# Scores of the first two pairs of heads as float32 in 64-row tiles, and small steps moved between engines

## The chip, the cores and the metric

The kernel runs on one core of a Trainium2 chip. The metric is the device time of one execution in microseconds (us). The program is written with an explicit order of instructions for each engine: TensorE (PE, with its weight loads PEld), VectorE (DVE), ScalarE (ACT), GpSimd (POOL) and SyncE (SP), which issues the DMAs.

## The reference, cut to what matters

```python
def _attn_ref(q, k, v, tau):                      # 8 batches, 8 heads, 576 rows, 64 wide
    scores = (1.0 / np.sqrt(64)) * np.matmul(q, k.transpose(0, 1, 3, 2))
    thresh = np.max(scores, axis=-1, keepdims=True) - tau
    scores = np.where(scores >= thresh, scores, -1e9)
    attn = np.exp(scores - np.max(scores, axis=-1, keepdims=True))
    attn = attn / (np.sum(attn, axis=-1, keepdims=True) + 1e-9)
    return np.matmul(attn, v)
def _moe_ref(x, mu_k, mu_r, w_k, w_v, w_r):       # x is 8 x 576 x 512, d_ff 1024
    xk = mu_k * x + (1 - mu_k) * x_prev           # x_prev: one row earlier
    xr = mu_r * x + (1 - mu_r) * x_prev
    k = np.maximum(xk @ w_k, 0.0)
    return 1 / (1 + np.exp(-(xr @ w_r))) * (k * k @ w_v)
def _moe2_ref(x, w_val, conv_w, w_out):           # causal convolution over 5 rows
    gate = 1 / (1 + np.exp(-conv(x, conv_w)))
    return gate * (x @ w_val) @ w_out
```

The five weight matrices and conv_w arrive as float64 and are converted on the chip.

## The kernel before, in words

**Attention.** The 64 heads are taken as 32 pairs; a pair has nine chunks of 128 query rows: eight of one head each (`c` from 0 to 7, the head alternating) and a ninth, `both`, that holds the last 64 rows of both heads. `prep` (from L392) loads q and k of a head with the 64 dimensions standing twice, on partitions 0 to 63 and 64 to 127. ScalarE rounds q (L409) and k (L405) to float32r, GpSimd subtracts in one half of the rows so that this half holds q's remainder (L419), and VectorE makes k's remainder `kl` (L413). The score of a chunk is then, for each half of the 576 keys (288), the sum of two float32r matmuls over all 128 rows, with k and with `kl` (`qk`, L462), into two PSUM banks. k carries the factor -1/8, so the scores are negated.

VectorE takes the minimum of the 576 scores of each row (L472), GpSimd adds tau to it (the threshold, L475), ScalarE exponentiates (L485), VectorE masks by the threshold and sums the row (L494). In the first six pairs (`LATE_PAIRS`) the sums of a half pair are collected in a tile `ss`; `guard_all` (L623, VectorE) adds 1e-9, `recip_all` (L628) inverts, GpSimd widens (L633), TensorE turns the result (L642) and the output is scaled (L647, L649). In the later pairs each chunk has its own guard (L499), reciprocal (L504) and a normalisation of P on GpSimd (L507).

P is transposed by TensorE. In pairs 0 to 3 (`COPY_FROM = 4`) directly, as float32 (L533); from pair 4 on a DMA first copies the P tile of two chunks into a tile `pr` (`move`, L561; two such tiles, `PRS`) and the transposes read that as float32r (L531). ScalarE brings the turned P back to SBUF (L544, L547, L552). TensorE multiplies it with V in float32: the two heads of a pair as two 64-column halves of the array (L597), the last keys of both in one piece (L600).

**Feed-forward.** `moe1` works on ten blocks of 464 rows: `mix_k` makes xk as a float32r value and a remainder, and the products with w_k and w_v are sums of three float32r matmuls (all at L674, in `mm3`). The first block needs the attention output of all four pairs of the first batch. `block2` does the same for w_r, w_val and w_out, with the convolution (L979), when the attention is over.

**Weights.** `split_weight` loads a 128 x 512 block of float64 as two 32-bit halves. `to_f32` (from L304) then makes a float32 of it in five steps: ScalarE scales the upper half read as float32 (L313), VectorE shifts it left by 3 (L316), VectorE puts the sign bit in (`sign`, L319), ScalarE scales the lower half (L323), GpSimd adds the two as integers (L326). ScalarE rounds the result to float32r (L353), and GpSimd or VectorE makes the remainder (L356). There are 28 such blocks: 8 of w_k and 8 of w_v early, 12 of the other three during the attention, and once a small one for conv_w.

**Order.** Nothing is scheduled by hand: every step is given to `Plan.op` with an engine, a guessed duration, its dependences and a priority, and `Plan.order` simulates the engines and buffers (tokens) and fixes the order in which each engine's instructions stand. All constants from L186 on are parameters of that plan: priorities and guessed durations. SyncE's one queue issues all loads, stores and copies in that order, and an issue that waits for its data holds back those behind it. The lines from L237 to L258 come ahead of the plan: the loads of `par` (identity, mixing factors, tau) and of `conv_w`, and a few small operations.

```python
    def op(self, eng, dur, fn, deps=(), prio=0.0, acq=(), rel=(), lat=0.0, port=False):
    ...
        deps = [last.get("qk")] + [o for hd in ((0, 1) if both else (head,)) for o in qk_done[pi, hd]]
    ...
        mx = op("dve", 670, least, (o,), e, acq=("sm",))
        th = op("pool", 260, thr, (mx,), at - THR_EARLY)
        e1 = chain("exp", op("act", 625, ex, (mx, last.get("exp")), e, acq=("p",) if head == 0 else ()))
        mk = op("dve", 821, mask, (e1, th), e, acq=("ss",) if late and c in (0, 4) else (),
```

## Time and profile before

| | |
|---|---|
| Time, median of 3 runs | 1241.86 us (1238.85 to 1243.0) |
| The profiled execution | 1238.36 us, span of its instructions 1236.5 us |
| Mean granted TensorE clock | 0.996 |
| Busy: PE, PEld | 1195.4 us (97%), 1015.8 us (82%) |
| Busy: DVE, ACT, POOL | 923.8 us (75%), 838.9 us (68%), 681.8 us (55%) |
| Chain that ended last | PE 77%, DVE 7%, DMA 6%, ACT 4%, POOL 3%, issue 3% |

The shares of the span are averages over stages that differ: attention of the first batch alone, attention beside the first feed-forward, and the second feed-forward alone. The matmul records are pipelined: a record lasts longer than the distance to the next one, so the pace is read from the starts. A line of the form "x16" in the timeline merges 16 instructions.

### The profile page before, as it was taken

How to read it: one execution, taken by the hardware profiler on the slowest of the kernel's cores; microseconds unless marked ns; L12 is line 12 of the kernel's file. 1: busy time of each engine (PE TensorE's matmuls, PEld its weight loads, DVE VectorE, ACT ScalarE, POOL GpSimd, SP SyncE). 2: the span in 40 equal slices, each digit the busy share in tenths (PEclk: the TensorE clock that was granted, in tenths of full speed). 3: DMA queues.
4: the chain of work that ended last, by engine and by line, in shares of the span. 5: the costliest groups of instructions: out<-in, count | busy, mean ns of one | idle time of the engine just before them, and what ended most of it. 6: DMA issues, size and time to landing. Idle time of an engine off the chain costs nothing.

```text
span 1236.5 us, 21250 instructions
## 1 busy us (share of the span) xinstructions
PE 1195.4 (97%) x7134; PEld 1015.8 (82%) x7134; DVE 923.8 (75%) x2029; ACT 838.9 (68%) x1609; POOL 681.8 (55%) x914
## 2 busy tenths in 40 slices
PE   5889999999999999999999999999999999999998
PEld 4667778887878788888887888888888888888887
DVE  7999988998888898798897876862425985555450
ACT  7899867887777776786876676753535775555442
POOL 5676766676566667566666474540306764444331
PEclk9989999999999999999999999999999999999999
DMA  7346545566646556555556455325106332221111
GB/s 251 119 145 229 205 175 214 206 234 234 230 168 227 214 204 227 195 185 206 210 203 237 158 180 179 151 114 202 63 16 238 109 123 93 93 93 64 38 38 62
DMA packets 71501, 201.91 MB, mean 163 GB/s; under 512 B 10848, under 2 KB 28384, under 8 KB 70624
## 3 DMA queue, kind: packets, MB, share of 16 engines
q1 hardware_dynamic: 71392, 200.55, 45.7%
q8 instruction: 57, 0.93, 0.3%
q14 instruction: 52, 0.43, 0.1%
HBM read 91.48 MB, written 34.73 MB: 102 GB/s over the span
## 4 chain that ended last, share of the span: by engine, by line
PE 77%; DVE 7%; DMA 6%; ACT 4%; POOL 3%; issue 3%; SPq 0%; DVEq 0%; POOLq 0%; ACTq 0%
PE g L674 51%; PE s L462 10%; PE g L597 8%; PE g L531 6%; DMA pr<-p 4%; PE g L600 3%; DVE p L494 2%; DVE sm L472 2%; ACT p L485 1%; DVE kl L413 1%; POOL sm L475 1%; POOL p L507 1%; ACT pt L544 1%; DMA raw<-in_qkb 0%; DMA stage<-in_w_r 0%
## 5 line engine op out<-in xcount | busy, mean ns | idle before, releaser
L507 POOL TENSOR_SCALAR p<-p,sm 128x576 f32<-128x576 f32 x234 | 192.3, 827 | 129.6 <-DVE sm L504 92.6
L472 DVE TENSOR_REDUCE sm<-s 128x1 f32<-128x576 f32 x288 | 212.2, 749 | 56.1 <-PE s L462 54.5
L485 ACT ACTIVATE p<-s,sm 128x576 f32<-128x576 f32 x288 | 211.5, 750 | 62.2 <-DVE sm L472 41.7
L494 DVE SCALAR_TENSOR_TENSOR p<-s,sm,p 128x576 f32<-128x576 f32 x288 | 229.1, 811 | 28.3 <-ACT p L485 18.6
L462 PE MATMUL s<-qkh 128*128 128x288 f32 x640 | 206.2, 337 | 14.5 <-ACT qkh L409 8.7
L462 PE MATMUL s<-kl,qkh 128*128 128x288 f32 x640 | 181.7, 299 | 0.1
L475 POOL TENSOR_SCALAR sm<-sm,gs 128x1 f32<-128x1 f32 x288 | 110.7, 386 | 107.2 <-DVE sm L472 62.9
L544 ACT ACTIVATE pt<-g 128x512 f32<-128x512 f32 x256 | 140.9, 603 | 29.4 <-PE g L531 27.5
L462 PEld LDWEIGHTS s<-qkh 128*128 128x128 f32 x640 | 122.7, 192 | 23.6 <-POOL qkh L419 9.2
L597 PE MATMUL g<-pt,v 128*64 128x320 f32 (+1 forms) x1024 | 139.7, 414 | 0.0
L531 PEld LDWEIGHTS g<-ident_r,pr 128*128 128x128 f32 (+1 forms) x1148 | 112.6, 140 | 19.4 <-issue 3.5
L462 PEld LDWEIGHTS s<-kl,qkh 128*128 128x128 f32 x640 | 123.0, 192 | 5.5 <-DVE kl L413 0.7
L531 PE MATMUL g<-ident_r,pr 128*128 128x128 f32 (+1 forms) x1148 | 118.6, 243 | 8.0 <-DMA pr<-p 7.0
L674 PE MATMUL g<-kh,w_v_hi 128*128 128x464 f32 x320 | 121.8, 380 | 0.0
L674 PE MATMUL g<-xkh,w_k_hi 128*128 128x464 f32 x320 | 120.9, 378 | 0.1
L674 PE MATMUL g<-xkh,w_k_lo 128*128 128x464 f32 x320 | 119.6, 374 | 0.0
L674 PE MATMUL g<-kh,w_v_lo 128*128 128x464 f32 x320 | 119.2, 372 | 0.0
L597 PEld LDWEIGHTS g<-pt,v 128*64 128x64 f32 x1024 | 68.8, 137 | 53.3 <-issue 11.5
L419 POOL TENSOR_TENSOR qkh<-raw,qkh 64x576 fp32r<-64x576 f32 x64 | 95.1, 1486 | 20.3 <-ACT qkh L409 8.6
L979 DVE SCALAR_TENSOR_TENSOR g<-y,cw_t,g 128x464 f32<-128x464 f32 x160 | 104.0, 700 | 1.2 <-ACT g L976 0.5
L937 DVE TENSOR_TENSOR y<-gate,vt 128x464 f32<-128x464 f32 x40 | 31.8, 801 | 74.8 <-ACT gate L932 73.4
L1011 POOL TENSOR_TENSOR gvl<-gate,gvh 128x464 fp32r<-128x464 f32 x40 | 48.3, 1208 | 70.2 <-ACT gvh L1008 70.2
(108 smaller groups left out, 2669.4 us busy)
## 6 DMA issues: line engine op xcount, KB each, us to landing
pr<-p SPq DMA_DIRECT2D x112, 576.0 KB, 3.5
raw<-in_qkb SPq DMA_DIRECT2D x32, 640.0 KB, 4.7
raw<-in_qka SPq DMA_DIRECT2D x32, 608.0 KB, 4.3
v<-in_vp SPq DMA_DIRECT2D x32, 320.0 KB, 3.1
x_d<-x SPq DMA_DIRECT2D x32, 290.0 KB, 4.0
v_d<-vo SPq DMA_DIRECT2D x40, 232.0 KB, 2.5
vt<-v_d SPq DMA_DIRECT2D x10, 928.0 KB, 4.6
pr<-p SPq DMA_DIRECT2D x28, 288.0 KB, 3.5
```

Source lines behind the costliest of these rows:

```text
L419: nc.gpsimd.tensor_tensor(out=t["hi"][lo_rows, qs], in0=t["raw"][lo_rows, qs], in1=t["hi"][lo_rows, qs].bitcast(F32), op=ALU.subtract)
L462: nc.tensor.matmul(s_t[g][:, hh, 0:NT], lhsT=q, rhs=k, start=(i == 0), stop=(i == len(terms) - 1))
L472: nc.vector.tensor_reduce(out=sm[:, 0:1], in_=s_t[g][:, :, 0:NT], op=ALU.min, axis=AX.XY)
L475: nc.gpsimd.tensor_scalar(out=sm_t[g][:, 1:2], in0=sm_t[g][:, 0:1], scalar1=tau_t, scalar2=1.0, op0=ALU.add, op1=ALU.mult)
L485: nc.scalar.activation(out=view(), in_=s_t[g][:, :, 0:NT], func=AF.Exp, bias=sm_t[g][:, 0:1], scale=-1.0)
L494: nc.vector.scalar_tensor_tensor(out=view(), in0=s_t[g][:, :, 0:NT], scalar=sm[:, 1:2], in1=view(), op0=ALU.is_le, op1=ALU.mult, accum_out=to)
L507: nc.gpsimd.tensor_scalar(out=view(), in0=view(), scalar1=sm_t[g][:, 3:4], scalar2=1.0, op0=ALU.mult, op1=ALU.mult)
L531: nc.tensor.transpose(o_.bitcast(F32R), in_=i_.bitcast(F32R), identity=ident_r)
L544: nc.scalar.activation(out=pt[:, head, :, q0:q0 + 128], in_=ps.rearrange("p (k q) -> p k q", k=4), func=AF.Copy)
L597: nc.tensor.matmul(acc[h * 64:h * 64 + 64, 0:n], lhsT=v[:, kc * 128 + h * 64:kc * 128 + h * 64 + 64], rhs=pt[:, h, kc, 0:n], start=(kc == ...
L674: nc.tensor.matmul(ps()[:, 0:TW], lhsT=W[w][wt][:, kc, m * 128:(m + 1) * 128].bitcast(F32R), rhs=a(at, kc), start=(i == 0 and x == 0), sto ...
L979: nc.vector.scalar_tensor_tensor(out=f["ps"], in0=t["y"][:, c, k:k + TW], scalar=cw[:, c, k:k + 1], in1=f["ps"], op0=ALU.mult, op1=ALU.add)
```

## The change: what it does, and the diff

- **Float32 scores.** For the first two pairs (`RAW_TO = 2`), q and k are loaded straight into the tile that TensorE reads, without rounding: q stands on both halves of the partitions as before, but on partitions 0 to 63 lies the first half of the keys and on 64 to 127 the second (the host lays that out), so only 288 or 352 columns of k are loaded and scaled. A chunk's scores are two float32 matmuls, each over 64 rows of the array, one on the upper and one on the lower rows (`qk_f32`). The four steps L409, L405, L413 and L419 fall away in these pairs; one scaling of k is left.
- **Signs.** In `to_f32` the shift falls away as a step of its own. GpSimd multiplies the upper half, read as float32, by zero, which leaves a signed zero (`zero`), and VectorE shifts and ors in one operation (`join`). The zero doesn't wait for ScalarE's scaling.
- **Guards.** `guard_all` goes from VectorE to GpSimd.
- **Copies.** `COPY_FROM` goes from 4 to 1: P of pairs 1 to 3 is copied too, and turned as float32r.
- **Loads.** `par` and `conv_w` are loaded from ScalarE's queue.
- **Plan.** Instructions have a mode, a change of mode costs `SWITCH` in the simulation, and chunks of the new mode may be ganged; the simulated DMA queue starts earlier; many constants have new values.

```diff
-EARLY, QK_EARLY, T_LATE, EV_EARLY, AV_LATE = 3.8603, 0.3303, -0.4166, 23.5198, 0.3289
+EARLY, QK_EARLY, T_LATE, EV_EARLY, AV_LATE = 4.2537, 0.3178, -0.4775, 98.9593, 0.4182
-MOE_LAG = 0.4706
-MOE_STEP = 0.8177
+MOE_LAG = 0.5251
+MOE_STEP = 0.8168
-COPY_FROM = 4
+COPY_FROM = 1
-MIX_EARLY, SIDE_EARLY = 4.2746, 0.1496
-W_KEY, W_STEP = -1.8366, 23.7965
-V_KEY, V_STEP = 1.1975, -0.1648
+MIX_EARLY, SIDE_EARLY = 6.4759, 0.2235
+W_KEY, W_STEP = 0.6869, 171.2624
+V_KEY, V_STEP = 1.6325, -0.7381
-VAL_LAG, OUT_LAG = 1.5867, 2.6821
-LATE2, LOAD2, MIX2, CONV_LAG, THR_EARLY = -0.8579, -49.8364, 0.8009, 207.2935, 184.052
-MIX_AT = 72.9433
-OUT_FETCH = 182.6794
-PORT_TOL, PORT_SLACK = 623.2361, 1.4633
+VAL_LAG, OUT_LAG = 2.8855, 4.4173
+LATE2, LOAD2, MIX2, CONV_LAG, THR_EARLY = 14.1984, 54.2671, 6.5168, 421.219, 1653.4806
+MIX_AT = 24.4154
+OUT_FETCH = 341.8965
+PORT_TOL, PORT_SLACK = 494.0914, 1.91
+SWITCH = 200.0
+GANG = 2.4021
+RAW_TO = 2
+DMA_FROM = 500.0
...
-    nc.sync.dma_start(out=par_t, in_=par)
+    nc.scalar.dma_start(out=par_t, in_=par)
...
-    nc.sync.dma_start(out=cw_raw, in_=conv_w)
+    nc.scalar.dma_start(out=cw_raw, in_=conv_w)
...
-        def shift():
-            nc.vector.tensor_scalar(out=bits, in0=fi, scalar1=3, scalar2=None, op0=ALU.logical_shift_left)
-
-        def sign():
-            nc.vector.scalar_tensor_tensor(out=bits, in0=fi, scalar=-2147483648, in1=bits,
-                                           op0=ALU.bitwise_and, op1=ALU.bitwise_or)
+        def zero():
+            nc.gpsimd.tensor_scalar(out=bits.bitcast(F32), in0=halves[:, :, 1].bitcast(F32), scalar1=0.0, scalar2=1.0,
+                                    op0=ALU.mult, op1=ALU.mult)
+
+        def join():
+            nc.vector.scalar_tensor_tensor(out=bits, in0=fi, scalar=3, in1=bits,
+                                           op0=ALU.logical_shift_left, op1=ALU.bitwise_or)
...
+        if pi < RAW_TO:
+            end = 640 + RAW_KW[head]
+
+            def load_f32():
+                t["hi"] = qk_t[pi, head] = qk_p.tile([128, w], F32R, name="qkh", tag="qkh")
+                nc.sync.dma_start(out=t["hi"][:, 0:end].bitcast(F32), in_=src[b, p][:, 0:end])
+
+            def scale_k():
+                k = t["hi"][:, 640:end].bitcast(F32)
+                nc.scalar.activation(out=k, in_=k, func=AF.Copy, scale=g_s)
+            o = dma(512 * end, load_f32, (), prio, acq=("qk",), more=700)
+            qk_done[pi, head] = (chain("cast", op("act", 400 + 53 * head, scale_k, (o, last.get("cast")), prio)),)
+            return
...
+        def qk_f32():
+            s_t[g] = (pool["s3"] if s_tok == "s3" else s_p).tile([128, 2, 512], F32, name="s", tag="s")
+            heads = (0, 1) if both else (head,)
+            for hd in heads:
+                t = qk_t[pi, hd].bitcast(F32)
+                q = (512, 0)[hd] if both else QO[hd] + j * 128
+                k = 640 + (64 if both and hd else 0)
+                for x in (0, 1):
+                    r = slice(64 * x, 64 * x + 64)
+                    nc.tensor.matmul(s_t[g][:, x, 0:NT], lhsT=t[r, q:q + 128], rhs=t[r, k:k + NT],
+                                     start=(hd == heads[0]), stop=(hd == heads[-1]))
...
                 def guard_all():
                     ss = ss_t[pi, half]
-                    nc.vector.tensor_scalar(out=ss[:, 0:n_s], in0=ss[:, 0:n_s], scalar1=1e-9, scalar2=1.0,
+                    nc.gpsimd.tensor_scalar(out=ss[:, 0:n_s], in0=ss[:, 0:n_s], scalar1=1e-9, scalar2=1.0,
                                             op0=ALU.add, op1=ALU.mult)
...
-                o = op("dve", 90, guard_all, masks, e, port=True)
+                o = op("pool", 240, guard_all, masks, e)
```

## Rows read from the trace of the kernel before

**Rows 1.** Windows of the core: stretch, length, busy PE, PEld, DVE, ACT, POOL, clock, DMA, GB/s.

```profile
0.00:11.10 11.10, 2.24 (x5) 1.31 (x5) 3.93 (x8) 5.58 (x9) 3.59 (x7) 1.00 0.77 262
11.10:44.00 32.90, 25.12 (x161) 20.00 (x160) 32.62 (x64) 29.90 (x57) 21.94 (x31) 1.00 0.61 201
44.00:113.30 69.30, 59.75 (x412) 45.97 (x412) 68.77 (x140) 61.41 (x121) 47.16 (x69) 0.95 0.48 165
113.30:310.00 196.70, 192.78 (x1263) 159.60 (x1264) 175.62 (x426) 153.67 (x302) 135.72 (x193) 0.99 0.60 210
310.00:1236.50 926.50, 915.49 (x5298) 788.94 (x5296) 642.82 (x1395) 588.29 (x1123) 473.36 (x615) 1.00 0.42 151
```

**Rows 2.** Timeline of PE, 100 to 125 us: start, duration, instruction; the first at L674.

```profile
113.28 0.48 PE L674 MATMUL g<-xkh,w_k_hi 128*128 128x464 f32 x1
```

**Rows 3.** Timeline of all engines, 0 to 22 us: the opening.

```profile
0.74 0.40 SPq L237 DMA_DIRECT2D par_t<-in_par  x1
...
1.66 0.42 SPq L402 DMA_DIRECT2D raw<-in_qka  x1
...
6.34 0.74 ACT L409 ACTIVATE qkh<-raw 128x640 fp32r<-128x640 f32 x1 [2.28 <-DMA raw<-in_qka]
...
8.67 0.61 PE L462 MATMUL s<-qkh 128*128 128x288 f32 x1 [8.67 <-ACT qkh L409]
...
11.11 0.74 DVE L472 TENSOR_REDUCE sm<-s 128x1 f32<-128x576 f32 x1
```

**Rows 4.** Groups by line and shape, whole span: count, busy us, mean ns, idle before.

```profile
L507 POOL TENSOR_SCALAR p<-p,sm 128x576 f32<-128x576 f32 x234 | 192.3, 827 | 129.6 <-DVE sm L504 92.6 <-DVE sm L499 35.2
...
L475 POOL TENSOR_SCALAR sm<-sm,gs 128x1 f32<-128x1 f32 x288 | 110.7, 386 | 107.2 <-DVE sm L472 62.9 <-DVE sm L499 15.7 <-ACT p L485 9.5
...
L419 POOL TENSOR_TENSOR qkh<-raw,qkh 64x576 fp32r<-64x576 f32 x64 | 95.1, 1486 | 20.3 <-ACT qkh L409 8.6 <-issue 6.2 <-POOL sm L475 1.8
...
L597 PE MATMUL g<-pt,v 128*64 128x320 f32 x512 | 76.8, 443 | 0.0
...
L597 PE MATMUL g<-pt,v 128*64 128x256 f32 x512 | 62.9, 385 | 0.0
...
L409 ACT ACTIVATE qkh<-raw 128x640 fp32r<-128x640 f32 x64 | 48.1, 751 | 4.4 <-DMA raw<-in_qka 2.3 <-PE s L462 1.7 <-DMA raw<-in_qkb 0.4
...
L405 ACT ACTIVATE qkh<-raw,gs 128x576 fp32r<-128x576 f32 x32 | 25.2, 788 | 0.0
```

**Rows 5.** Windows of L316 alone (the shift): stretch, length, DVE busy, clock, DMA, GB/s.

```profile
11.10:113.30 102.20, 9.99 (x12) 0.97 0.52 176
```

**Rows 6.** Windows of L623 alone (the guard on VectorE), the same columns.

```profile
11.10:113.30 102.20, 5.24 (x9) 0.97 0.52 176
```

**Rows 7.** Windows of L413 alone (the remainder of k), the same columns.

```profile
11.10:113.30 102.20, 10.20 (x11) 0.97 0.52 176
```

**Rows 8.** The tile pr, 95 to 160 us: its copies by DMA, from issue to landing.

```profile
DMA to landing us min/median/max: 2.3/3.7/7.2
```

**Rows 9.** Timeline of PE, 20 to 100 us: scores, products with V, scores.

```profile
57.23 0.29 PE L462 MATMUL s<-qkh 128*128 128x288 f32 x1
57.37 0.29 PE L462 MATMUL s<-kl,qkh 128*128 128x288 f32 x1
57.59 2.38 PE L597 MATMUL g<-pt,v 128*64 128x320 f32 x16
59.89 0.81 PE L600 MATMUL g<-ptl,v 128*128 128x320 f32 x2
60.30 0.54 PE L462 MATMUL s<-qkh 128*128 128x288 f32 x1
60.67 0.30 PE L462 MATMUL s<-kl,qkh 128*128 128x288 f32 x1
```

**Rows 10.** Timeline of PE: eight transposes as float32 (L533) and as float32r (L531).

```profile
68.95 1.04 PE L533 MATMUL g<-par_t,p 128*128 128x128 f32 x8
...
117.37 0.84 PE L531 MATMUL g<-ident_r,pr 128*128 128x128 f32 x8
```

More of the change, by code (lines that the diff above doesn't have):

```diff
@@ L46 @@
 QKW = (KO[0] + KW[0], KO[1] + KW[1])
+RAW_KW = (288, 352)
 NCH = 9
@@ L88, in order @@
         n = 0
-        port = 0.0
+        port, mode = 0.0, 0
         cold, runs = True, []
-        busy["dma"] = 1400.0
-        heapq.heappush(events, (1400.0, -1, "idle", None))
+        busy["dma"] = DMA_FROM
+        heapq.heappush(events, (DMA_FROM, -1, "idle", None))
         def push(t, kind, o):
@@ L139, in order @@
                             skipped.append(held)
+                    if e == "pe" and mode == 1 and pick is not None and pick.mode != 1:
+                        late = pick.prio + GANG
+                        while ready[e]:
+                            x = heapq.heappop(ready[e])
+                            if x[2].mode == 1 and x[0] <= late and all(free[t] > 0 for t in x[2].acq):
+                                skipped.append((pick.prio, pick.idx, pick))
+                                pick = x[2]
+                                break
+                            skipped.append(x)
+                            if x[0] > late:
+                                break
                     for x in skipped:
@@ L157, in order @@
                     if e == "pe":
+                        if pick.mode != mode:
+                            pick.dur += SWITCH
+                        mode = pick.mode
                         while runs and runs[0][1] < now - WARM:
@@ L326, in add @@
             nc.gpsimd.tensor_tensor(out=bits, in0=bits, in1=fi, op=ALU.add)
-        return scale, shift, sign, low, add
+        return scale, zero, join, low, add
     for f in to_f32(cw_raw, cw_t[:, 0, :].bitcast(I32), cw_t[:, 1, :]):
@@ L1064 @@
     qkb = np.concatenate([bb, bb], 2)
+    kr = np.concatenate([kb[..., 512:], kb], -1)
+    for i in range(RAW_TO):
+        i = divmod(i, NP)
+        for x in (0, 1):
+            qka[i][64 * x:64 * x + 64, 640:640 + RAW_KW[0]] = ka[i][:, x * NT:x * NT + RAW_KW[0]]
+            qkb[i][64 * x:64 * x + 64, 640:640 + RAW_KW[1]] = kr[i][:, x * NT:x * NT + RAW_KW[1]]
     vp = np.zeros((B, NP, 128, 640), f)
```

22 lines of the change are left out of this document (15 added, 7 removed).

## The prediction, made before the changed kernel ran

> **What bounds the kernel now.** I read the windows of the whole core first [rows 1]. From 113.3 us to the end TensorE is busy for 192.8 + 915.5 of 1123.2 us: all that can be won there is 14.9 us of gaps, spread over the whole rest. Up to 113.3 us it is busy for 2.24 + 25.12 + 59.75 = 87.1 us and idle for 26.2 us. The same rows say why: between 11.1 and 113.3 us VectorE is busy for 32.62 + 68.77 = 101.4 of 102.2 us, 99%. ScalarE is next with 91.3 us (89%), GpSimd has 69.1 us (68%). So the first stage is VectorE's, the rest is TensorE's, and the border is the first matmul of the first feed-forward block at 113.28 us [rows 2]; it needs the attention output of all four pairs of the first batch. An edit that shortens VectorE's queue ahead of that matmul moves everything behind it; one that saves VectorE time later saves nothing.
>
> Inside the first stage the opening is a stretch of its own [rows 3]: the first load of q and k is issued third on SyncE's queue, at 1.66 us; ScalarE starts to cast it at 6.34, so it took 4.7 us for 608 KB with other loads in flight. The first score matmul runs at 8.67 us, VectorE's first reduction of a finished score at 11.11 us.
>
> **The opening.** The loads of par and conv_w go to ScalarE's queue. That puts two issues of about 0.4 us ahead of ScalarE's first work, covered by its wait for the loads. The first q/k load then takes the slot at 0.74 us. It shrinks from 608 to 464 KB; if all 4.7 us scale with bytes it takes 3.6 us, if none do 4.7 us, so it lands between 4.3 and 5.4. One ScalarE scaling of k follows. There is no row of 288 or 352 columns; half of the 576-column one's 788 ns [rows 4] is the floor, the whole the ceiling, and I take 0.5 us. Then the first scores: the first F32R matmul lasts 0.61 us [rows 3], about twice those below, and a F32 chunk needs three such steps at worst (below), 1.8 us. The reduction starts between 6.6 and 7.8 us; I take 7.1, **4.0 us earlier** (bounds 3.3 to 4.5).
>
> **VectorE's list ahead of 113.3 us.** Removed: the shift, 12 times, 9.99 us [rows 5]; the guard, 9 times, 5.24 us [rows 6], 0.58 us each for five numbers a row, so most of it is waiting; the remainder of k of the second pair, 2 of 11 at 10.20 / 11 = 0.93 us [rows 7], 1.9 us. Those of the first pair lie in the opening. Sum **17.1 us**. Nothing is added: the joined shift-and-or replaces the old second operation one for one. By VectorE alone the border would move by 4.0 + 17.1 = 21 us, to 92 us. Something else is late before that.
>
> **ScalarE is next.** It does 5.58 + 29.90 + 61.41 = 96.9 us of work before the border [rows 1]. For two pairs, four casts of q (0.75 us) and four of k (0.79 us) go [rows 4], and four scalings of 0.5 us come: minus 4.2 us, leaving 92.7 us, from about 4.8 us on. Packed without a gap it ends at 97.5 us; at its present 89% at 109.0. VectorE, when it was the bound, reached 99%; I take 97% for ScalarE, 95.6 + 4.8 = 100.4 us.
>
> **The copies of P.** From the second pair on each P tile goes through a DMA before it is transposed. Between 95 and 160 us such a copy lands in 2.3 to 7.2 us, median 3.7 [rows 8]. For most chunks this is latency beside other chunks' work. It is exposed once, at the last chunk of the fourth pair, which gates the border: **plus 3.7 us**, so 104.1 us. It adds 12 copies of 576 KB and 3 of 288 KB, 7.8 MB, in a stage that moves 165 to 201 GB/s [rows 1]; over some 75 us that is 104 GB/s more, and SyncE's queue, which issues the weights' loads as well, gets 15 more issues. I cost that at nothing more; the slower rival is its price if the cover fails.
>
> **TensorE in the first stage.** F32 matmuls are in the trace: the products of P with V. Their records last 443 ns at 320 columns and 385 at 256 [rows 4], 58 / 64 = 0.91 ns a column, yet 16 of 320 columns start within 2.30 us [rows 9], 144 ns each: two run at once, on two column halves of the array. The change puts two on two row halves, which this trace doesn't show. A score of 288 columns is 0.26 us an instruction, four to a chunk: 0.52 us if pairs overlap fully, 0.79 us for a chunk alone (in program order the second half's first instruction starts beside the first half's second), 1.05 us if nothing overlaps; today four F32R matmuls at a pace of 0.14 us take 0.53 us [rows 9]. Two pairs hold 20 such units (eight single chunks and one double for each). Entering and leaving the split array costs 0.22 - 0.14 and 0.37 - 0.14 us [rows 9], 0.31 us together. The Trainium skill, in TensorEngine Tiling, Key Properties, says that changing the tiling mode, not just the tile, drains TensorE; that speaks against short runs of such tiles, gives no figure, and the two gaps agree with it; by that rule, with every unit alone, TensorE's work below would be 95.4 us, still covered. If half of the units stand alone: 10 x (0.26 + 0.31) = 5.7 us more. The transposes of 27 chunks become F32R: eight take 0.84 instead of 1.04 us [rows 10], 25 ns each, 123 times, minus 3.1 us. TensorE's work ahead of the border goes from 87.1 to 89.7 us, in 104.1 - 5.5 = 98.6 us: covered, with 9 us to spare (bounds 84 to 101 us). Without that cover it is the second rival.
>
> **GpSimd** loses four remainders of q at 1.49 us [rows 4], 5.9 us. It gets 13 products with zero; the nearest row is the normalisation of 576 columns at 827 ns, so 0.74 us for 512 if it scales, and double that if the stride of the float64 halves hurts; I take 0.74, 9.6 us. It gets 9 guards at the 386 ns of its other small operation [rows 4], 3.5 us. 72.7 - 5.9 + 9.6 + 3.5 = 79.9 us of 104: off the path as a sum. But its thresholds (one for each chunk) stand in the same queue, VectorE's mask waits for them, and the next reduction stands behind that mask. VectorE's reciprocal now waits for a guard on GpSimd in the same way.
>
> **After the border** the plan's other constants move, loads and priorities among them, and the 12 later weight blocks lose a VectorE step that TensorE hides. I cost this at nothing, with the 14.9 us of gaps as the measure of what it could do either way.
>
> **Sum.** The border moves from 113.3 to 104.1 us: minus 9.2 us. The profiled execution took 1238.4 us (span 1236.5), so 1229.2; the median of the runs shown is 3.5 us above it, so **1232.5 us** in terms of the median. With ScalarE at 100% it is 1229.8, at 89% 1241; with the opening's bounds 0.7 either way. What a measurement of this kernel can tell from no change is about 0.3%, 3.7 us: faster is below 1238.1, slower above 1245.6.
>
> **Rivals.**
> *The row halves don't overlap.* Then 20 units cost 0.53 us more and, with a switch at each, TensorE has 87.1 + 10.6 + 6.2 - 3.1 = 100.8 us ahead of the border; at 97% from 5.5 us on it ends at 109.4: minus 3.9 us, **1238**. For it: no row shows row halves. Against it: the column halves do overlap.
> *GpSimd's queue takes VectorE's place.* If every product with zero stands in front of a threshold that VectorE waits for, 13 x 0.74 = 9.6 us come back: **1242**. For it: four engines would then be at 77% or more, and GpSimd's weight steps run 1.3 us at a time. Against it: GpSimd had a third of the stage free, and its four long remainders of q go.
> *The copies bound the stage; slower.* P's copy has two tiles, each held from the issue until 18 transposes (some 1.9 us) are done. At 3.7 us to land a tile turns every (3.7 + 1.9) / 2 = 2.8 us; the stage needs one for two chunks, 4.5 us (44 chunks in 98 us). It decides from a landing of 7.1 us on. With weights, q, k and copies together on the DMA engines at 10 us to land, each of 13.5 tiles costs 1.5 us too much, 20 us: **1252**. For it: 7.2 us occurs already. Against it: the median is half of that, and DMA is at 0.48 to 0.61 [rows 1].
> *The new constants undo it later.* If the gaps after the border grow by two thirds, 10 us come back: **1242**; if they shrink by a third, 1227.5.
>
> **Chances.** Forecast 0.60 (nearly all of it faster), no overlap 0.12 (two thirds faster), GpSimd 0.12 (0.05 faster, 0.05 same, 0.02 slower), copies 0.07 (nearly all slower), constants 0.09 (0.03 each). Faster 0.58 + 0.08 + 0.05 + 0.03 = 0.74, same 0.15, slower 0.11. The range goes from 1225 (ScalarE packed, the granted clock of 0.95 from 44 to 113.3 us [rows 1] back at 1.00, later gaps a little smaller) to 1242, which leaves out the copies, the worse halves of GpSimd and of the constants, and some 0.05 below.
>
> **What would show it.** First score matmul near 5 us, first reduction near 7; the shift gone from VectorE and the guard on GpSimd; the first feed-forward matmul near 104 us; VectorE below 95% and ScalarE above 93% before it; TensorE's idle time ahead of the border down from 26 to 12 to 17 us, and about 15 us behind it. Score instructions of the first two pairs starting 0.13 us apart on average say that halves overlap, 0.26 that they don't. I am wrong if the border stays at 110 us or more, or if it moves and the gaps behind it grow by as much.

## The result and the profile after

The changed kernel takes 1245.98 us (median of 15 runs, 1244.17 to 1252.83) against 1240.28 for the kernel before (15 runs beside them, 1236.81 to 1243.79): a ratio of 1.0054, 95% interval 1.0041 to 1.0067. It is slower by about 0.5%, where 1232.5 us was forecast. The profiled execution took 1244.49 us, its span is 1242.7.

I cut both spans at the same two events: the first score matmul, and the first matmul of the first feed-forward block, the border of [rows 2]. "Stage" is what lies between them, "rest" what comes behind. The windows view of the kernel before over stage and rest (columns as in [rows 1]):

```profile
8.67:113.30 104.63, 87.10 (x576) 67.27 (x576) 103.62 (x204) 92.72 (x179) 70.86 (x101) 0.97 0.53 181
113.30:1236.50 1123.20, 1108.27 (x6559) 948.54 (x6559) 818.45 (x1820) 741.96 (x1424) 609.08 (x808) 1.00 0.45 161
```

The same view of the changed kernel, with the opening:

```profile
0.00:13.16 13.16, 0.00 (x0) 0.00 (x0) 0.62 (x5) 2.51 (x6) 0.64 (x6) 1.00 0.86 310
13.16:118.50 105.34, 90.44 (x584) 62.48 (x584) 97.25 (x192) 94.48 (x187) 81.10 (x124) 0.95 0.67 240
118.50:1242.70 1124.20, 1108.09 (x6553) 946.70 (x6551) 807.67 (x1795) 729.61 (x1414) 604.12 (x815) 1.00 0.45 160
```

The 6.2 us between the spans are 13.16 - 8.67 = 4.5 in the opening, 0.7 in the stage and 1.0 in the rest. So the loss stands nearly whole before the first score. The second surprise is the stage: VectorE is busy for 6.4 us less in it (97.25 for 103.62), and it did not get shorter.

The opening, in the timeline of the changed kernel (start, duration, engine, instruction, and in brackets the idle time before it and what ended that):

```profile
0.74 0.40 SPq L449 DMA_DIRECT2D qkh<-in_qka  x1
0.74 0.41 ACTq L256 DMA_DIRECT2D par_t<-in_par  x1
...
5.41 0.31 ACT L259 ACTIVATE ident_r<-par_t 128x128 fp32r<-128x128 f32 x1 [2.94 <-DMA par_t<-in_par]
5.41 0.35 ACTq L263 DMA_DIRECT2D cw_raw<-in_conv_w  x1
11.92 0.22 ACT L332 ACTIVATE cw_t<-cw_raw 128x20 f32<-128x20 f32 x1 [6.20 <-DMA cw_raw<-in_conv_w]
...
12.59 1.00 ACT L453 ACTIVATE qkh<-qkh,gs 128x288 f32<-128x288 f32 x2
...
13.16 2.42 PEld L508 LDWEIGHTS s<-qkh 64*128 64x128 f32 x12 [13.16 <-ACT qkh L453]
13.16 2.77 PE L508 MATMUL s<-qkh 64*128 64x288 f32 x10 [13.16 <-DMA v<-in_vp]
14.54 0.76 DVE L523 TENSOR_REDUCE sm<-s 128x1 f32<-128x576 f32 x1 [2.11 <-PE s L508]
```

Read it as one queue. ScalarE's program is: load par, make ident_r of it (L259), load conv_w, convert conv_w (L332), scale k (L453). Both loads are issued by this queue, in this order. The load of conv_w is therefore not issued until par has landed, at 5.41 us; its 20 KB, now behind the bulk loads, land 6.5 us later. The scaling of k stands behind, and the first score waits for it: its weight load starts when the scaling (L453) ends. (The bracket of the matmul itself names a load of v, which had landed before that; the weight load of the same matmul names the scaling.) The first loads of q and k, issued at 0.74 us and after, landed 4.5 to 5.3 us later and lay waiting. The reduction starts at 14.54 us, where [rows 3] have 11.11 and I forecast 7.1.

What the change was to do on TensorE, it did. The PE timeline of the changed kernel, a single chunk (x4, two instructions for each half of the keys) and a run of four chunks (x16):

```profile
23.20 0.76 PE L508 MATMUL s<-qkh 64*128 64x288 f32 x4
23.89 0.77 PE L584 MATMUL g<-par_t,p 128*128 128x128 f32 x5
...
27.88 2.21 PE L508 MATMUL s<-qkh 64*128 64x288 f32 x16
30.02 1.09 PE L584 MATMUL g<-par_t,p 128*128 128x128 f32 x8
```

Sixteen score instructions start within 30.02 - 27.88 = 2.14 us, 134 ns each: the two row halves of the array work at once. A chunk alone takes 23.89 - 23.20 = 0.69 us up to the next instruction.

New operations by line and shape, whole span (count, busy, mean ns, idle before):

```profile
L453 ACT ACTIVATE qkh<-qkh,gs 128x352 f32<-128x352 f32 x2 | 1.2, 585 | 0.0
L453 ACT ACTIVATE qkh<-qkh,gs 128x288 f32<-128x288 f32 x2 | 1.0, 522 | 0.0
...
L335 POOL TENSOR_SCALAR stage<-stage 128x512 f32<-128x512 f32 x20 | 14.4, 721 | 8.2 <-DMA stage<-in_w_v 5.8 <-DMA stage<-in_w_out 0.8 <-DMA stage<-in_w_r 0.8
...
L674 POOL TENSOR_SCALAR ss<-ss 128x4 f32<-128x4 f32 x6 | 2.4, 406 | 3.2 <-DVE p L545 2.9
```

These prices were forecast as 0.5 us, 0.74 us and 0.386 us.

### The profile page after: what moved, and what is told of

Its sections match the earlier page's. It is cut to its first block, busy times and chain, and to the rows that moved or that the text cites. A ratio compares the mean times of both kernels' runs of the same rounds, so it can differ in the third digit from the quotient of the medians.

```text
span 1242.7 us, 21266 instructions
## 1 busy us (share of the span) xinstructions
PE 1198.5 (96%) x7134; PEld 1009.2 (81%) x7134; DVE 905.5 (73%) x1991; ACT 826.6 (67%) x1605; POOL 685.9 (55%) x944
## 5 line engine op out<-in xcount | busy, mean ns | idle before, releaser
L558 POOL TENSOR_SCALAR p<-p,sm 128x576 f32<-128x576 f32 x234 | 186.4, 802 | 135.4 <-DVE sm L555 96.3
L498 PE MATMUL s<-qkh 128*128 128x288 f32 x600 | 191.2, 334 | 5.8 <-DVE p L545 4.6
L498 PE MATMUL s<-kl,qkh 128*128 128x288 f32 x600 | 169.0, 296 | 0.0
L526 POOL TENSOR_SCALAR sm<-sm,gs 128x1 f32<-128x1 f32 x288 | 107.5, 375 | 101.8 <-DVE sm L523 69.2
L582 PE MATMUL g<-ident_r,pr 128*128 128x128 f32 (+1 forms) x1271 | 135.5, 244 | 13.9 <-DMA pr<-p 5.5
L582 PEld LDWEIGHTS g<-ident_r,pr 128*128 128x128 f32 (+1 forms) x1271 | 125.8, 140 | 27.8 <-ACT pt L595 6.9
L498 PEld LDWEIGHTS s<-qkh 128*128 128x128 f32 x600 | 113.4, 189 | 15.3 <-DVE p L545 3.8
L498 PEld LDWEIGHTS s<-kl,qkh 128*128 128x128 f32 x600 | 114.0, 190 | 4.4
L442 POOL TENSOR_TENSOR qkh<-raw,qkh 64x576 fp32r<-64x576 f32 x60 | 90.8, 1513 | 18.3 <-ACT qkh L432 12.7
L801 POOL TENSOR_TENSOR xrl<-xf,xrh 128x464 fp32r<-128x464 f32 x40 | 50.6, 1280 | 63.4 <-ACT xrh L798 63.1
```

Of the source, the lines that this page charges most:

```text
L442: nc.gpsimd.tensor_tensor(out=t["hi"][lo_rows, qs], in0=t["raw"][lo_rows, qs], in1=t["hi"][lo_rows, qs].bitcast(F32), op=ALU.subtract)
L498: nc.tensor.matmul(s_t[g][:, hh, 0:NT], lhsT=q, rhs=k, start=(i == 0), stop=(i == len(terms) - 1))
L526: nc.gpsimd.tensor_scalar(out=sm_t[g][:, 1:2], in0=sm_t[g][:, 0:1], scalar1=tau_t, scalar2=1.0, op0=ALU.add, op1=ALU.mult)
L558: nc.gpsimd.tensor_scalar(out=view(), in0=view(), scalar1=sm_t[g][:, 3:4], scalar2=1.0, op0=ALU.mult, op1=ALU.mult)
L582: nc.tensor.transpose(o_.bitcast(F32R), in_=i_.bitcast(F32R), identity=ident_r)
```

## The experiments

All kernels in one table, by the windows view cut as above: first score, length of the stage, busy VectorE, ScalarE and GpSimd in it, granted clock in it, length of the rest; then the ratio to the kernel before with its interval. "Old order" means that the instruction order is that of the kernel before, "new order" that of the changed one; an edit in such a kernel changes or moves single instructions and leaves all others where they stand. In three kernels (marked *) the plan is computed anew, so the whole order differs.

| kernel | first score | stage | VectorE | ScalarE | GpSimd | clock | rest | ratio |
|---|---|---|---|---|---|---|---|---|
| before | 8.67 | 104.6 | 103.6 | 92.7 | 70.9 | .97 | 1123.2 | 1 |
| b3_loads_act, old order | 13.93 | 104.3 | 103.5 | 92.1 | 70.7 | .97 | 1124.6 | 1.0056 [1.0036, 1.0076] |
| b1_signs, old order | 8.66 | 110.0 | 100.2 | 92.6 | 77.1 | .92 | 1125.0 | 1.0056 [1.0033, 1.0079] |
| b2_guards, old order | 8.78 | 105.1 | 100.9 | 92.2 | 73.7 | .94 | 1125.6 | 0.9992 [0.9971, 1.0012] |
| b4_signs_guards_cw, old order | 8.30 | 104.5 | 94.6 | 92.6 | 80.5 | .95 | 1130.6 | 1.0027 [1.0009, 1.0045] |
| c4_guards_cw, old order | 7.98 | 103.5 | 100.1 | 92.6 | 73.5 | .95 | 1125.3 | 0.9990 [0.9976, 1.0003] |
| c2_relief, old order | 8.42 | 103.8 | 103.2 | 90.7 | 70.4 | .95 | 1123.7 | 0.9989 [0.9975, 1.0002] |
| c1_relief_full, old order | 7.68 | 104.9 | 97.5 | 90.9 | 80.3 | .97 | 1132.5 | 1.0014 [1.0001, 1.0027] |
| d1_all, old order | 8.60 | 103.1 | 101.8 | 90.5 | 73.4 | .98 | 1125.7 | 0.9999 [0.9983, 1.0016] |
| d2_all_par, old order | 7.66 | 104.5 | 101.9 | 90.4 | 74.0 | .95 | 1122.2 | 0.9993 [0.9976, 1.0010] |
| after | 13.16 | 105.3 | 97.3 | 94.5 | 81.1 | .95 | 1124.2 | 1.0054 [1.0041, 1.0067] |
| e1_loads_sync, new order | 6.27 | 108.2 | 97.7 | 95.2 | 80.6 | .92 | 1126.0 | 1.0018 [0.9998, 1.0039] |
| c3_cw_late, new order | 5.64 | 106.8 | 97.3 | 95.2 | 81.3 | .94 | 1126.8 | 1.0022 [1.0006, 1.0037] |
| e8_start, new order | 11.12 | 106.4 | 97.3 | 94.5 | 81.2 | .94 | 1126.2 | 1.0061 [1.0041, 1.0082] |
| e5_act_twice, new order | 6.23 | 110.8 | 98.4 | 103.5 | 81.1 | .97 | 1125.5 | 1.0041 [1.0021, 1.0061] |
| e7_pool_twice, new order | 6.44 | 110.6 | 100.0 | 95.9 | 89.7 | .89 | 1130.1 | 1.0065 [1.0043, 1.0087] |
| e6_old_signs, new order | 6.04 | 107.3 | 100.9 | 95.7 | 71.9 | .95 | 1131.2 | 1.0068 [1.0045, 1.0091] |
| e3_copy4 * | 12.83 | 98.3 | 92.0 | 88.0 | 75.5 | .95 | 1139.3 | 1.0116 [1.0087, 1.0146] |
| e2_old_consts * | 12.67 | 103.9 | 94.2 | 93.5 | 81.6 | .95 | 1144.8 | 1.0226 [1.0190, 1.0263] |
| e2r_new_consts * | 8.26 | 96.9 | 94.1 | 86.9 | 69.0 | .98 | 1149.2 | 1.0149 [1.0119, 1.0179] |

Lengths and busy times are of one profiled execution each, the ratio is of all runs; the runs of one kernel lie several microseconds apart (1236.8 to 1243.8 for the kernel before, above), so where the two disagree by as much, the ratio decides. Each ratio is to runs of the kernel before on the same chip. The kernels' lines are shifted by a few against those of before and after.

**The loads.** Theory: the two small loads on ScalarE's queue are the loss. Rival: the loss comes from the rest of the change and the late start is made up for later. First the changed kernel with both loads back on SyncE's queue:

```diff
-    nc.scalar.dma_start(out=par_t, in_=par)
+    nc.sync.dma_start(out=par_t, in_=par)
...
-    nc.scalar.dma_start(out=cw_raw, in_=conv_w)
+    nc.sync.dma_start(out=cw_raw, in_=conv_w)
```

> The changed kernel with the loads of par and conv_w back on SyncE's queue, ahead of q and k; nothing in the plan's order changes. Theory A (late loads: on ScalarE's queue conv_w's load is issued only after par has landed, lands at 11.9 us, and the conversion of conv_w stands ahead of the first scaling of k, so the first score comes at 13.2 us instead of 8.7, and this start carries the loss): first score at 6 to 7.5 us, time 5 to 7 us lower, 1239 to 1241 us. Theory B (the copies of P hold the first stage) and theory C (the order made by the new constants loses later): first score earlier all the same, but the first feed-forward matmul stays within 2 us of 118.5 us and the time within 2 us of the changed kernel's.

Measured 1241.23 us, 1.0018: about two thirds of the loss are gone, and the interval holds 1. Then the reverse, the kernel before with nothing but the two loads moved to ScalarE's queue:

> The kernel before with the loads of par and conv_w on ScalarE's queue alone. Theory A (conv_w's issue waits for par, its data come behind the bulk loads, and its conversion stands ahead of the casts): first score at 11 to 13 us instead of 8.7, time 3 to 5 us over before, 1243 to 1246 us. If the start were hidden: within 1.5 us of before.

Measured 1245.09 us, 1.0056: the move alone costs what the whole change costs. The opening of that kernel, in its timeline:

```profile
0.74 0.40 ACTq L237 DMA_DIRECT2D par_t<-in_par  x1
...
5.61 0.33 ACTq L244 DMA_DIRECT2D cw_raw<-in_conv_w  x1
10.75 0.22 ACT L313 ACTIVATE cw_t<-cw_raw 128x20 f32<-128x20 f32 x1 [4.84 <-DMA cw_raw<-in_conv_w]
...
11.62 0.72 ACT L409 ACTIVATE qkh<-raw 128x640 fp32r<-128x640 f32 x1
...
13.93 0.61 PE L462 MATMUL s<-qkh 128*128 128x288 f32 x1 [13.93 <-POOL qkh L419]
```

The same chain with the old conversion of q and k; its stage is as long as before's (104.3 and 104.6 us), so the 5.3 us of the opening go straight to the end. Which of the two loads it is, c3_cw_late shows: the changed kernel with par left on ScalarE's queue, and conv_w loaded (from SyncE's queue) and converted halfway through the program:

> The changed kernel with one edit: conv_w's load and conversion issued halfway through the program instead of at the start (par stays on ScalarE's queue, the first load of q and k stays first on SyncE's). Theory L (the loss is conv_w's load, whose data the ScalarE queue waits for before the first scaling): par lands at 5.4 us, the first score runs at 6.3 to 7, the time comes out at 1239.5 to 1241.5, as with both loads back on SyncE's queue. If par's slow load alone delays the start, or the rest of the new order costs the time, the first score comes later than 10 us, or the time stays at 1244 or more.

Its opening, in the timeline:

```profile
4.53 0.31 ACT L259 ACTIVATE ident_r<-par_t 128x128 fp32r<-128x128 f32 x1 [2.09 <-DMA par_t<-in_par]
...
5.05 0.54 ACT L454 ACTIVATE qkh<-qkh,gs 128x288 f32<-128x288 f32 x1 [0.21 <-DVE gs L276]
...
5.64 3.51 PE L509 MATMUL s<-qkh 64*128 64x288 f32 x12 [5.64 <-ACT qkh L454]
...
7.01 0.76 DVE L524 TENSOR_REDUCE sm<-s 128x1 f32<-128x576 f32 x1 [2.00 <-PE s L509]
```

With conv_w out of the way the opening is what I had forecast for the change: first score near 5, first reduction 7.0 (forecast 7.1). It is conv_w that costs the 7.5 us from 5.64 to 13.16 in the opening. The time, though, is 1242.63 us, 1.0022: against the kernel before, the opening is 3.0 us earlier, the stage 2.1 longer, the rest 3.6 longer. I had expected 1239.5 to 1241.5; the start is earlier than expected and less of it arrives. (Halfway through, ScalarE waits 1.7 us for conv_w to land; that is in the rest.)

One try missed its aim. e8_start takes par from SyncE's queue, conv_w halfway, and issues the first loads of q and k from ScalarE's queue:

```diff
-    nc.scalar.dma_start(out=par_t, in_=par)
+    nc.sync.dma_start(out=par_t, in_=par)
...
-                nc.sync.dma_start(out=t["hi"][:, 0:end].bitcast(F32), in_=src[b, p][:, 0:end])
+                (nc.sync if pi or head else nc.scalar).dma_start(out=t["hi"][:, 0:end].bitcast(F32), in_=src[b, p][:, 0:end])
```

> Run e1 with the start shortened further: par first on SyncE's queue, q and k of the first head from ScalarE's queue, conv_w loaded and converted halfway through the program. First score at 5.2 to 5.7 us instead of 6.3. Theory A (the start moves all behind it): 0.5 to 1 us below e1, 1240 to 1241 us.

Measured 1247.92 us, 1.0061, first score at 11.12: I had repeated the error under test. The load of q and k now stood behind ident_r in ScalarE's queue, and so behind the landing of par: it was issued at 2.73 us, by then behind the bulk loads of the other queue, and the scaling that waits for it starts at 10.53.

**What sets the stage: parts alone.** In the old order, the new signs alone, the guards alone, and both with conv_w halfway (which clears the opening of its conversion):

```diff
-            nc.vector.tensor_scalar(out=bits, in0=fi, scalar1=3, scalar2=None, op0=ALU.logical_shift_left)
+            nc.gpsimd.tensor_scalar(out=bits.bitcast(F32), in0=halves[:, :, 1].bitcast(F32), scalar1=0.0, scalar2=1.0,
+                                    op0=ALU.mult, op1=ALU.mult)
...
-                    nc.vector.tensor_scalar(out=ss[:, 0:n_s], in0=ss[:, 0:n_s], scalar1=1e-9, scalar2=1.0,
+                    nc.gpsimd.tensor_scalar(out=ss[:, 0:n_s], in0=ss[:, 0:n_s], scalar1=1e-9, scalar2=1.0,
```

> The kernel before, in its own order, with the new signs alone: GpSimd's product with zero in the place of the shift, the joined shift-and-or in the place of the sign. VectorE loses 10 us ahead of the first feed-forward matmul, where it is 99% busy; GpSimd gains some 9 us. Theory G (VectorE's list is the bound, as the prediction said): stage 5 to 9 us shorter, time 1232 to 1236 us. Theory H (the engines wait for each other in a fixed order, and ScalarE at 88 to 90% is as full as it gets): within 3 us of before, 1237 to 1243 us.

> The kernel before, in its own order, with the first six pairs' guards on GpSimd alone. VectorE loses 5.2 us ahead of the first feed-forward matmul, most of it waiting; GpSimd gains 3.5 us. Theory G: 3 to 5 us below before, 1235 to 1238 us. Theory H: within 3 us of before, 1238 to 1243 us.

> The kernel before with the new signs and guards in its own order, and conv_w loaded and converted halfway through the program, so that q and k are issued one place earlier (first score at 8.0 to 8.4 us). Theory G: 8 to 14 us below before, 1226 to 1233 us. Theory H: 0 to 3 us below before, 1237 to 1241 us.

The signs alone cost 0.56%, the guards alone nothing measurable, both together (with conv_w halfway) 0.27%. Neither theory had b1 or b4 slower than before. b4's stage in the windows view:

```profile
8.30:112.80 104.50, 89.16 (x576) 69.16 (x576) 94.57 (x182) 92.56 (x180) 80.52 (x121) 0.95 0.55 180
```

VectorE is busy for 94.6 us instead of 103.6, 90% instead of 99%, and the stage lasts 104.5 us instead of 104.6. That is the forecast's central sentence with its premise met and its conclusion missing. But b1 and b4 hand VectorE's work to GpSimd, so they don't relieve VectorE alone. In b1 new waits stand in VectorE's rows (waits view, its stage, VectorE; the kernel before has only the first of these, and 0.2 us of p behind GpSimd's sm):

```profile
DVE kl L414 <- ACT qkh L406: 4.3, 2, 4.1
DVE sm L473 <- PE s L463: 3.2, 6, 1.3
DVE p L495 <- POOL qkh L420: 1.6, 1, 1.6
DVE stage L320 <- POOL stage L316: 1.3, 1, 1.3
DVE p L495 <- POOL sm L476: 1.0, 2, 0.8
DVE wst L320 <- POOL wst L316: 0.6, 1, 0.6
```

In b4's stage VectorE waits for GpSimd for 6.4 us by the same view (2.4 for the guards, 4.0 for thresholds, q's remainder and weight steps), where the kernel before has 0.2: two thirds of the 9 us that it was relieved of. That much of my rival "GpSimd's queue takes VectorE's place" is there in the old order. In the changed kernel's stage these waits are 1.7 us. No run relieves VectorE without giving the work to another engine.

**What sets the stage: load on one engine.** Two reliefs that don't hang on the change. c2_relief is the kernel before with the small evacuations of P's last key tile (0.29 us each on ScalarE) on VectorE in the first four pairs; c1_relief_full is the same edit in b4:

```diff
-                nc.scalar.activation(out=pt_t[pi, c // 4][1][:, q0:q0 + 128], in_=tps[g, 1][:, 0:128], func=AF.Copy)
+                if pi < 4:
+                    nc.vector.tensor_copy(out=pt_t[pi, c // 4][1][:, q0:q0 + 128], in_=tps[g, 1][:, 0:128])
+                else:
+                    nc.scalar.activation(out=pt_t[pi, c // 4][1][:, q0:q0 + 128], in_=tps[g, 1][:, 0:128], func=AF.Copy)
```

> The kernel before with one edit: the same evacuations (128x128, 0.29 us, eighteen in the stage) on VectorE for the first four pairs. Theory V (the prediction's: VectorE's 99% is the bound): VectorE gets about 18 x 0.2 to 0.3 = 3.6 to 5.2 us more and the border moves from 113.3 to 117 or 118, the time to about 1244. Theory S (ScalarE): the border comes 3 to 5 us earlier, time about 1236. Theory E: within 2 us of 113.3, time within 2.5 us of before.

> The kernel before with its own order, the new signs and the guards on GpSimd, conv_w loaded halfway (as the run b4_signs_guards_cw), and in addition the eighteen-odd 128x128 evacuations of P's last key tile (0.29 us each, 5.2 us of ScalarE in the stage) move to VectorE for the first four pairs. Theory S (ScalarE is next in line once VectorE has 9 us to spare): the stage shrinks by about 5 us against 104.5, to 99.5, and the time by 4 to 5 us against 1242.8, to about 1238.5. Theory E (the engines wait for each other in a fixed order, no one engine's total sets the length): the stage moves by less than 2 us, the time stays within 1240 to 1245.

c2 in the windows of its stage, and the moved instruction among VectorE's groups there:

```profile
8.42:112.20 103.78, 89.76 (x576) 69.69 (x576) 103.16 (x220) 90.68 (x164) 70.44 (x101) 0.95 0.54 183
```

```profile
L553 DVE COPY ptl<-g 128x128 f32<-128x128 f32 x16 | 4.4, 274 | 0.0
```

An engine that is busy for 99% of the stage takes 4.4 us of work more, its busy time stays at 103.2, and the stage is not longer (103.8 for 104.6; time 0.9989). So those 99% were not a full engine. (The edit also takes 2.0 us off ScalarE's busy time; that could hide a cost of VectorE only if the two cancelled, and VectorE's rows show where the 4.4 us went: into the guards, 3.1 us for 5.3, and the remainders of k, 12.2 for 13.3, among others.) Nor is ScalarE next in line: with VectorE relieved and ScalarE 2 us shorter, c1's stage is 104.9 us.

Then doses in the other direction, on the changed kernel with its loads on SyncE's queue (e1): the first instruction of each weight conversion on ScalarE, or the product with zero on GpSimd, done twice. That repeats an instruction in place and changes nothing of what is computed.

```diff
-                b["f"] = to_f32(b["raw"], t[:, 1024:1536].bitcast(I32), t[:, 1536:2048].bitcast(F32))
+                f = list(to_f32(b["raw"], t[:, 1024:1536].bitcast(I32), t[:, 1536:2048].bitcast(F32)))
+                if keep:
+                    f[0] = lambda g=f[0]: (g(), g())
+                b["f"] = f
```

> The changed kernel with the loads on SyncE's queue (run e1: 1241.2 us, first feed-forward matmul at 114.5 us), and ScalarE's first weight step done twice for the 16 blocks of w_k and w_v; the order of all else stays. It adds 14 x 0.67 = 9.3 us of ScalarE before the first feed-forward matmul. Theory D (ScalarE holds the first stage, at some 90% busy, so VectorE's relief bought nothing): that matmul 7 to 10 us later, time 6 to 9 us over e1. Theory F (VectorE still holds it): within 2 us of e1. Theory E (no engine alone: the queues wait for each other in turn): 3 to 5 us over e1, and about the same for the other two doses.

> Run e1 with GpSimd's product with zero done twice for the 16 blocks of w_k and w_v: 14 x 0.7 = 10 us more on GpSimd before the first feed-forward matmul. Theories D and F: within 2 us of e1. Theory E: 3 to 5 us over e1. If GpSimd's queue holds the stage: 7 to 10 us over e1.

ScalarE gets 103.5 - 95.2 = 8.3 us more and the stage 2.5; GpSimd gets 9.1 more and the stage 2.3. Neither is a bound, where a microsecond costs a microsecond. By the ratios e7 costs 0.47% over e1, clear of the noise; e5's 0.23% is not.

**Signs back on VectorE in the new order** (e6: e1 with the shift and the sign's extraction on VectorE, no product with zero):

> Run e1 with the signs made as before: shift and sign on VectorE, nothing on GpSimd, everything else in e1's order. It gives VectorE back some 14 x 0.7 = 10 us before the first feed-forward matmul and takes 10 us from GpSimd. Theory D: VectorE has 10 us free there, so 0 to 3 us over e1. Theory F: 8 to 10 us over e1. Theory E: 3 to 5 us over e1. If GpSimd's added work were what holds the stage, 3 us or more below e1.

Measured 1.0068 against e1's 1.0018. So in the new order the old signs cost 0.5%, and in the old order the new signs cost: b1 against before 0.56%, b4 against c4 0.37%, c1 against d1 0.15% (this last one within the noise). The same edit is good in the order made with it and bad in the other.

**The plan's constants.** The changed kernel with the old constants, the old kernel with the new ones (priorities and lags), and the changed kernel with P copied from the fifth pair on, as before (COPY_FROM = 4):

> The changed kernel with the plan's priorities and lags of before (EARLY to PORT_SLACK, and 1400 for the start of the simulated DMA queue); all edits of the work stay. Theory C: 3 to 5 us lower, 1241 to 1243 us, and the gaps of TensorE behind the first feed-forward matmul shrink from 18 to about 15 us. Theories A and B: within 2 us of the changed kernel, 1244 to 1248 us, first score still at 13 us.

> The kernel before with the new priorities and lags alone. Theory C: 3 to 5 us slower than before, 1243 to 1246 us. Theories A and B: within 2 us of before, 1238 to 1242 us.

> The changed kernel with P copied from the fifth pair on, as before. Theory B: the first feed-forward matmul comes 4 to 6 us earlier than 118.5 us and the time falls by 3 to 6 us, to 1240 to 1243 us. Theory A: no more than 2 us either way, 1244 to 1248 us. Theory C: any change comes behind the first feed-forward matmul, not ahead of it.

Ratios 1.0226, 1.0149 and 1.0116, all to the kernel before; against the changed kernel's 1.0054, e2 is 1.7% slower and e3 0.6%. All three lie outside what any of the theories gave. Each of these computes a new order from constants that came with the other kernel, so none isolates its edit. But they say something of the border. Of e2r, in the windows:

```profile
8.26:105.20 96.94, 80.19 (x521) 62.17 (x522) 94.07 (x191) 86.90 (x170) 68.97 (x93) 0.98 0.54 177
105.20:1254.40 1149.20, 1123.78 (x6615) 958.53 (x6613) 832.79 (x1838) 743.52 (x1433) 606.56 (x811) 0.99 0.45 159
```

Its first feed-forward matmul comes 8.1 us earlier than before's, and its time is 1.49% longer: 55 matmuls that the kernel before runs ahead of the border run behind it, and gaps come with them (1149.2 - 1123.8 = 25.4 us, for 14.9). e3's border, too, comes 7.4 us earlier than the changed kernel's, with 58 matmuls fewer ahead of it, and its time is longer. The border is one point of an interleaved order, and to pull it forward is no gain by itself. What part the copies of P and the float32 scores have in the time could not be had alone in this way; that stays open.

**A version that beats both.** Three small edits that each measured 0.1% or nothing in the old order: guards on GpSimd with conv_w halfway (c4), then with c2's evacuations (d1), then with par's load on ScalarE's queue, so that q and k are loaded first (d2):

> The kernel before with its own order, signs as before, the guards on GpSimd and conv_w's load and conversion halfway. A try for a version that beats both: the opening takes no conversion of conv_w, first score at about 8.3 instead of 8.7 us, and VectorE loses the guards' 5 us. Theory V: border 5 us earlier, about 1234. Theory E: 0 to 1 us gained, 1238.5 to 1240.5; the part of the signs' cost that the run b4_signs_guards_cw shows (1242.8) then belongs to the product with zero on GpSimd.

> The kernel before with three small edits together: guards on GpSimd, conv_w's load and conversion halfway, the 128x128 evacuations of the first four pairs on VectorE. Each pair of them alone measured 0.9989 to 0.9992. If what they free adds up: border at about 110.5 us, 0.998, some 1238. Theory E (the order holds the stage): 0.999 again, no measurable difference.

> The same with par's load on ScalarE's queue, which leaves the first load of q and k first on SyncE's, as in the changed kernel. The first cast of q should start near 5.1 instead of 5.6 us and the first score near 7.3; a gain in the opening of 0.5 us that should show in full, 1237.5, if the stage behind it is a fixed length, and not at all if the stage lengthens by what the opening gives, as the run c3_cw_late has it (opening 3.0 us earlier than before's, border 0.9 us earlier).

Ratios 0.9990, 0.9999 and 0.9993; all intervals hold 1. There is no gain to be measured, and none of the kernels tried beats the kernel before by more than the measurement is uncertain.

## Why the prediction was wrong

**The opening, the step that decides the result.** "That puts two issues of about 0.4 us ahead of ScalarE's first work, covered by its wait for the loads." I counted the issues and not where the second stands: behind an instruction that waits for the first load. The step was costed at nothing in an opening that was to gain 3.7 us at the first score (8.67 to near 5); it gave a loss of 4.5. The new signs' conversion, the scale and the first scores are not to blame: with conv_w out (c3) the first reduction starts at 7.0 us, 0.1 from the forecast. That the loads are the cause of the opening's loss is shown from both sides (e1, b3). None of my rivals named them; the slower side came true by a step that I had taken for free. I had also taken the old landing times for granted. Ahead of the bulk loads on one queue conv_w lands 1.9 us after its issue (kernel before); issued later, from another queue, it took 6.5 (changed kernel) and 5.1 (b3). The Trainium skill, in DMA: Bandwidth & Descriptors, "Issuing engines are not separate DMA queues", says that transfers from all engines run on the same 16 DMA engines and interleave, and that a second issuer saves issue time only; these landings agree with that.

**"An edit that shortens VectorE's queue ahead of that matmul moves everything behind it."** This is the step that would have failed even with a good opening. 99% busy was read as full; it isn't. c2 puts 4.4 us more into it at no cost, b4 takes 9.0 us out at no gain. My list had a hint that I used for the guard alone ("0.58 us each for five numbers a row, so most of it is waiting"). Records overlap (VectorE's groups in the stage of before, by the lines view, sum to 117.9 us in 104.6), and some hold waiting. The timeline of the kernel before shows for what; guards (L623), shifts (L316) and what GpSimd ran beside them:

```profile
34.19 0.42 DVE L316 TENSOR_SCALAR stage<-stage 128x512 int32<-128x512 int32 x1
...
52.56 2.09 DVE L623 TENSOR_SCALAR ss<-ss 128x5 f32<-128x5 f32 x1
...
53.36 1.26 POOL L326 TENSOR_TENSOR wst<-wst 128x512 int32<-128x512 int32 x1
...
58.98 1.30 POOL L356 TENSOR_TENSOR w_k_lo<-wst,w_k_hi 128x512 fp32r<-128x512 f32 x1 [1.15 <-ACT w_k_hi L353]
...
59.17 1.39 DVE L316 TENSOR_SCALAR stage<-stage 128x512 int32<-128x512 int32 x1
...
62.69 0.15 DVE L623 TENSOR_SCALAR ss<-ss 128x4 f32<-128x4 f32 x1
```

The guard that starts at 52.56 us ends at 54.65, 0.03 us after GpSimd's sum; the shift that starts at 59.17 ends at 60.56, 0.28 us after GpSimd's remainder. So it goes in the whole stage: six of the nine guards end 0.02 to 0.03 us after a GpSimd instruction that ran when they began, the other three take 0.15 to 0.16 us; the shifts that begin beside such an instruction end about 0.28 us after it and last 0.57 to 1.58 us, the others take 0.41 to 0.42. At these shortest times twelve shifts and nine guards are an estimated 6.5 us of work; the other 8.8 of the 15.2 us that I took off VectorE's list go by until GpSimd is done. (In e6 fourteen shifts take 0.42 us each, so giving them back cost VectorE 5.9 us and not the 10 expected.) Such waiting can shrink when other work comes (c2) and move to other records when its instruction goes (in b4 the remainders of k take 14.9 us for 13.3). No run of its own tests this reading. The sum of durations on a queue is then no price of leaving one out. The Trainium skill, in Perfetto Trace Analysis, "Identifying the Most-Contended Engine", takes the engine of highest occupancy as the one to optimise first, and for VectorE takes occupancy as a fair measure of how close it is to its roofline, too; in this stage the measurement differs, and it decides.

**"ScalarE is next", packed to 97%.** ScalarE's work before the border was forecast at 92.7 us and came to 2.51 + 94.48 = 97.0, as much as before: in the new order 40 instead of 33 weight steps (5.0 us more by their records) and 45 instead of 44 exponentials stand ahead of the border, and some of its operations run longer there. And nothing packs: its busy share of the stage is between 84 and 90% in all kernels of either fixed order but the dosed e5 (93%). The forecast stage of some 99 us would have needed the engines to fill each other's waits by themselves. In these fixed orders they didn't.

**"Nothing is added" on VectorE.** Wrong in size too: the new order gives it three remainders of xk that GpSimd made before, and does more of the weights ahead of the border. Among VectorE's groups in the changed kernel's stage:

```profile
L801 DVE TENSOR_TENSOR xkl<-xf,xkh 128x464 fp32r<-128x464 f32 x3 | 3.0, 987 | 0.1
L376 DVE TENSOR_TENSOR w_k_lo<-wst,w_k_hi 128x512 fp32r<-128x512 f32 x2 | 2.2, 1094 | 0.2
...
L376 DVE TENSOR_TENSOR w_v_lo<-stage,w_v_hi 128x512 fp32r<-128x512 f32 x1 | 0.7, 697 | 0.0
```

That is 5.9 us of remainders; with one more chunk and 14 joined steps in the place of 11 (2.1 us), VectorE's busy time before the border fell from 1.70 + 103.62 to 0.62 + 97.25 us, 7.5 instead of 17.1.

**The copies of P.** "Plus 3.7 us, exposed once", at the last chunk ahead of the border, is not shown: the one copy that TensorE waited for in the changed kernel's stage stands 27 us ahead of the border, in the timeline of PE,

```profile
91.62 0.84 PE L582 MATMUL g<-ident_r,pr 128*128 128x128 f32 x8 [1.81 <-DMA pr<-p]
```

That wait is 1.8 us; ScalarE's exponentials waited twice more, 1.0 us together, for a P tile that a copy still held. The 20 copies issued between 30 and 118 us landed in 2.3 to 7.9 us, median 3.5, so the slower rival's price (10 us to land) was not reached, and the median is half of its condition (7.1 us).

**After the border**, costed at nothing with 14.9 us of gaps as the measure: TensorE's work there is the same (1108.1 and 1108.3 us), the gaps are 16.1. Right in the changed kernel. (The expectation of e2 speaks of 18 us; the windows give 16.1.) But the constants are worth much: exchanged, they cost 1.5% in the old kernel (e2r) and 1.7% in the changed one (e2).

**What held.** Row halves overlap (134 ns, forecast 0.13), so that rival fell; a lone chunk takes 0.69 us to the next instruction (forecast 0.79 with a switch of 0.31 counted apart; the switch is inside the 0.69); TensorE's work ahead of the border is 90.4 us (forecast 89.7) and stayed covered, though it goes with the granted clock (89.5 us at .97 in e5, 93.3 at .92 in e1); GpSimd's work there is 0.64 + 81.10 us (forecast 79.9); the prices of the scaling, the zero and the guard. The range's low end also took the granted clock of the stage back to 1.00; it was .95. The sum itself has a slip: 1229.2 and 3.5 us are 1232.7, not 1232.5. A sum whose prices are right can have the wrong sign: they were right for new operations, and the time was in what stands before what.

## What to carry to other kernels

A DMA issue is an instruction of its engine's queue: before moving one, write out what stands ahead of it there and what that waits for, and what stands behind it and waits for its data. A busy share near 100% names a suspect, not a bound; put a few microseconds of extra work on that engine, or take some away, and see whether the stage moves, before building on it. A record that is long for its shape may hold a wait for another engine: compare it with the shortest of its kind, and look at what ended when it ended. In a fixed order of instructions like this one, relief on one engine was swallowed and the parts of a change did not add up: the signs were worth something only in the order made with them. A loss in the opening, ahead of the whole order, went straight to the end (b3); a gain there did not (c3 starts 3.0 us earlier than the kernel before and takes no less time).

## What was unexpected of the hardware

In the kernel before, VectorE's shifts and guards that begin beside a GpSimd instruction last until it has ended: 0.15 us for a guard that meets none, 2.09 for one that does. A small transfer's time depends on what it stands behind: the 20 KB of conv_w took 1.9 us ahead of the bulk loads, 6.5 behind them, and 2.8 halfway through the program (c3). TensorE's granted clock in the stage lies between .89 and .98 in kernels that run the same 576 matmuls there or nearly so, and its busy time goes with it: 87.1 us at .97 (before), 92.3 at .92 (b1). The mean is a mixture of stretches at either of its two levels, 1.2 and 2.4 GHz (in the kernel before 1.00 up to 74 us and .50 from 76 to 82, after TensorE had stood idle from 74 to 76). A stage with a lower clock need not be longer (c4: .95 and 103.5 us); whether the longer stages with the lowest clocks (b1 110.0 at .92, e7 110.6 at .89) are its cause or its effect was not settled.
